# Loading q and k of the first three blocks in 512-byte pieces, and turning them head by head with the identity

## The chip, the core and the metric

The kernel runs on one core of one Trainium2 chip. The metric is the device time of one execution in microseconds (us). The core has five engines that run their own instruction queues in order: TensorE (PE, with its weight loads shown apart as PEld), VectorE (DVE), ScalarE (ACT), GpSimd (POOL) and SyncE (SP), which here issues nearly all DMAs.

## The reference

Three layers in a row. First an attention over 4 x 8 heads, 576 tokens, 64 columns a head, in which each token sees itself and the 63 before it; then a dense layer whose activation is a quotient of polynomials; then a layer of 8 experts, one per token.

```
scores = (1/8) * q @ k.T ;  rel = row - column ;  scores = where(0 <= rel < 64, scores, -1e9)
x  = softmax(scores) @ v                       # 2304 tokens x 512
h  = x @ w_in ;  g = P(h) / (Q(|h|) + 1e-6) ;  x = g @ w_out      # 512 -> 2048 -> 512
e  = argmax(x @ w_gate) ;  out = p[e] * sigmoid(x @ w_output_gate)[e] * relu(x @ w1[e]) @ w2[e]
```

q and k are float32, and the weights come as float64.

## The kernel before

The 2304 tokens are cut into nine blocks of 256 (`TB`). Attention works in units n = 4u + c: block u, and pair c of the eight heads. For two pairs at a time, m = n // 2 (block u, half g of the heads), `load_qk` (line 318) brings k and q into tiles of [128 partitions, 2, 4 heads, 64]: partition p and place t hold token 128t + p of the block. SP issues one DMA for each of k and q and each t; its pieces are the 64 floats of one token and head, 256 bytes. The first m is split into two pairs of heads more, which gives eight DMAs of 64 KB in place of four of 128 KB. In block 2 a sequence ends after 64 tokens, so its t = 0 takes two DMAs of 64 partitions.

`at_T` (line 407) turns a unit: four PE transposes (k and q, t = 0 and 1), each of a [128 tokens, 2 heads x 64] piece against the identity, into one PSUM tile `tq` of [128, 2, 2, 128]. Two evictions (`evac`, ACT or DVE) copy the k half into `kT`, and the q half, scaled, into `qT`, 256 tokens in a row for each of 128 head columns. kT and qT are parts of the one constant tile that the trace calls KK, so the evictions show as `KK<-tq`. Then `at_QK` (line 433) makes the scores: eight float32 matmuls a unit of 64 x 64 against 128 columns (`sc`); `soften` adds the mask (DVE), takes exponents (ACT) and scales (POOL, `ms<-ms,rs`); `at_PT` turns the result (`pp`, four transposes) and `at_PV` multiplies with v (`xp`, eight float32 matmuls of 128 x 64 against 64 columns).

Beside that run the conversion of w_in and w_out from float64 bits (`stg` -> `cp`, `ct` on DVE -> `wi`, `wo` on ACT and POOL) and the dense layer's first steps (`h`, `y`). All instructions from the start to step 12 (`S_TAPE`) of the dense layer are recorded by the class `Tape` and played in the order written out by hand in `ORDER` (line 36). That order fixes for each engine, SP too, what follows what, and for instructions with a choice the engine. The played instructions stand in the profile under line 124, all others under line 96. The units of the first three blocks (n = 0 to 11, u below `NG` = 3) and of block 3 lie in the played part; it ends on PE at about 84 us.

The order on PE around the turns is: turns 0 and 1, scores of 0 and 1; turns 2 and 3, `pp` of 0, scores of 2, `pp` of 1; turn 4, `xp`, scores, turn 5; later turns 6 and 7, then 8 and 9, then 10 and 11, with `xp`, `sc`, `pp` and `h` between them.

Of the kernel before, what the change touches and what calls it, by code (L numbers as in the profile page):

```python
# [23 lines left out]
NQ, TA, VU = 4, 2, 2  # L24
# [3 lines left out]
NG, HF = 3, 4  # L28
# [102 lines left out]
def kernel(  # L131
# [16 lines left out]
    nc = Tape(tc.nc)  # L148
    B, H, S, D = q.shape
# [3 lines left out]
    W = 64  # L153
    TB = 256
# [16 lines left out]
    scale = 1.0 / float(D) ** 0.5  # L171
# [33 lines left out]
    qT = [cols["qT"][:, i * TB:(i + 1) * TB] for i in range(NQ)]  # L205
    kT = [cols["kT"][:, i * (W + TB):(i + 1) * (W + TB)] for i in range(NP)]
# [3 lines left out]
    ident = cs[:, C_ID:C_ID + 128]  # L210
    qc_col = cs[:, C_QC:C_QC + 1]

    def t2(shape, name, dt=F32):
        return s2.tile(shape, dt, tag="s2", name=name)
# [7 lines left out]
    def pt(shape, name):  # L222
        return ps.tile(shape, F32, tag=name, name=name)
# [15 lines left out]
    def pick(**cost):  # L239
        e = min(cost, key=lambda x: load[x] + cost[x])  # L240
        load[e] += cost[e]
        return e

    def dve(n, fast=False):
        return 0.07 + n / (1920.0 if fast else 960.0)

    def act(n):
        return ACT0 + n / 1200.0
# [4 lines left out]
    def evac(o, i, n, mul=None):  # L253
        e = pick(D=dve(n), A=act(n))
        if mul is None:
            nc.either(e, D=lambda: nc.vector.tensor_copy(out=o, in_=i), A=lambda: nc.scalar.copy(out=o, in_=i))
        else:
            nc.either(e, D=lambda: nc.vector.tensor_scalar(out=o, in0=i, scalar1=mul, scalar2=None, op0=ALU.mult),
                      A=lambda: nc.scalar.mul(out=o, in_=i, mul=mul))
# [48 lines left out]
    def runs(t0, n):  # L308
        done = 0
        while done < n:  # L310
            b, s = divmod(t0 + done, S)
            step = min(n - done, S - s)
            yield done, step, b, s
            done += step
# [3 lines left out]
    def load_qk(m):  # L318
        u, g = divmod(m, 2)
        for nm, dst in (("k", k_t), ("q", q_t)):  # L320
            dst[m] = t2([128, 2, 4, D], nm)
        step = 4 if m else 2
        for h0 in range(0, 4, step):
            for src, dst in ((k, k_t[m]), (q, q_t[m])):
                for t in range(2):
                    for off, n, b, s in runs(u * TB + t * 128, 128):
                        h = 4 * g + h0
                        nc.sync.dma_start(out=dst[off:off + n, t, h0:h0 + step],
                                          in_=src[b, h:h + step, s:s + n, :].rearrange("h p d -> p h d"))
            if m == 0 and h0 == 0:  # L330
                nc.sync.dma_start(out=cs[:, C_MASK:], in_=cst[:, C_MASK:C_QC + 1])

# [74 lines left out]
    def at_T(n):  # L407
        nc.mark()
        u, c = divmod(n, NP)
        tq = pt([128, 2, 2, 128], "tq")  # L410
        cc = 2 * (c % 2)
        for a, src in ((0, k_t[n // 2]), (1, q_t[n // 2])):
            for r in range(2):
                nc.tensor.transpose(tq[:, a, r, :], src[:, r, cc:cc + 2, :].rearrange("p h d -> p (h d)"), ident)
        if u:
            e = pick(D=dve(W, True), A=act(W), G=0.2)
            nc.either(e if e == "G" else "D", G=lambda: nc.gpsimd.tensor_copy(out=kT[c][:, :W], in_=kT[c][:, TB:]),
                      D=lambda: nc.vector.tensor_copy(out=kT[c][:, :W], in_=kT[c][:, TB:]))
        evac(kT[c][:, W:], tq[:, 0].rearrange("d r p -> d (r p)"), TB)
        evac(qT[n % NQ], tq[:, 1].rearrange("d r p -> d (r p)"), TB, -scale)  # L420

    def mask(u, j):
        i = 4 * u + 2 * j
# [635 lines left out]
    def qk_upto(m):  # L1059
        while loaded[0] <= min(m, NUNIT // 2 - 1):  # L1060
            load_qk(loaded[0])
            loaded[0] += 1
# [8 lines left out]
    for n in range(NUNIT + 2):  # L1071
        first, second = [], []
        if n < NUNIT and (group(n) == 1 or n % 2):
            first.append((at_QK, n))
        if n % 2 and n > 2 and group(n - 2) == 2:
            first.append((at_PV, n - 2))
        if n + TA < NUNIT:
            second.append((at_T, n + TA))
        while done < min(n, NUNIT) and (group(done) == 1 or n % 2 == 0):
            first.append((at_PT, done))  # L1080
            if group(done) == 1:
                second.append((at_PV, done))
            done += 1
        evs += [first, second]
# [91 lines left out]
    for n in range(TA):  # L1176
        at_T(n)
# [158 lines left out]
```

## Time and profile before

| | us |
|---|---|
| median of 3 runs (753.07 to 754.02) | 753.62 |
| the profiled execution, its time | 752.35 |
| the profiled execution, its span (first to last instruction) | 750.60 |
| PE busy in the span | 726.9 |
| DVE, ACT, POOL busy | 509.9, 444.8, 461.7 |

PE busy counts instructions whose ends are modelled; a wait is what a view shows as idle time ahead of an instruction. A share of the DMA engines over 100% means that packets overlap in an engine.

### The profile page before, as it was taken

The numbers are of one execution on the slowest core, as the hardware profiler recorded it, in microseconds if no ns is written. First come the engines' busy times: TensorE is split into PE (matmuls) and PEld (weight loads), VectorE is DVE, ScalarE is ACT, GpSimd is POOL, SyncE is SP. The second block draws the span as 40 slices with busy tenths as digits, with TensorE's granted clock in tenths as the row PEclk, the third lists the DMA queues.
The fourth block names the chain that finished last, engine by engine and source line by source line (L and its number), as shares of the span: only waits on it lengthen the run. The fifth ranks groups of instructions, "written<-read, shape, count | busy, mean of one in ns | idle before, by whom it ended". The sixth has DMA issues, their size and how long they took to land.

```text
span 750.6 us, 14603 instructions
## 1 busy us (share of the span) xinstructions
PE 726.9 (97%) x5288; PEld 641.9 (86%) x5288; DVE 509.9 (68%) x1262; ACT 444.8 (59%) x1001; POOL 461.7 (62%) x390
## 2 busy tenths in 40 slices
PE   4889999999999999999999999999999999999996
PEld 3677998889899899899899999998888888888886
DVE  4999999987887867767767777798386622235111
ACT  4999776998577577577677566676531402223020
POOL 3588686665465665465475375577862867666451
PEclk9999999999999999999999999999999999999998
DMA  9999502433222022122121001146506545412410
GB/s 194 307 264 302 164 1 85 138 85 83 84 58 58 21 62 53 27 61 57 31 56 30 1 30 30 69 133 198 190 3 252 181 156 182 141 71 108 159 38 25
DMA packets 96865, 78.56 MB, mean 105 GB/s; under 512 B 74703, under 2 KB 75215, under 8 KB 96784
## 3 DMA queue, kind: packets, MB, share of 16 engines
q1 hardware_dynamic: 92944, 67.77, 30.9%
q0 software_dynamic: 3840, 9.76, 3.9%
q8 instruction: 44, 0.72, 0.4%
q14 instruction: 37, 0.30, 0.1%
HBM read 66.25 MB, written 11.53 MB: 104 GB/s over the span
## 4 chain that ended last, share of the span: by engine, by line
PE 84%; DMA 5%; DVE 4%; SPq 2%; ACT 2%; POOL 1%; issue 1%; POOLq 0%; DVEq 0%; ACTq 0%
PE y L96 20%; PE h L96 20%; PE hp L96 14%; PE yp L96 14%; PE h L124 3%; PE y L124 2%; SPq L124 2%; DMA q<-in_q_dram 2%; PE xp L96 1%; DVE t L96 1%; PE pp L96 1%; PE sc L96 1%; PE ytp L96 1%; DMA stg<-in_moe_w_out_dram 1%; PE lt L96 1%
## 5 line engine op out<-in xcount | busy, mean ns | idle before, releaser
L96 PE MATMUL y<-wo,g 128*128 128x512 f32 x768 | 190.1, 396 | 0.0
L96 PE MATMUL h<-xh,wi 128*128 128x256 f32 x896 | 171.7, 284 | 0.5 <-DVE mn L96 0.3
L96 PEld LDWEIGHTS y<-wo,g 128*128 128x128 f32 x768 | 139.6, 188 | 27.3 <-issue 0.2
L96 PEld LDWEIGHTS h<-xh,wi 128*128 128x128 f32 x896 | 143.6, 191 | 3.0 <-ACT ms L96 0.5
L96 PE MATMUL h<-xl,wi 128*128 128x256 f32 x448 | 127.5, 285 | 0.0
L96 POOL TENSOR_TENSOR wx<-wr,wx 128x1024 fp32r<-128x1024 f32 x44 | 107.0, 2460 | 26.6 <-DVE wx L96 17.8
L96 PE MATMUL yp<-wx,hT 128*128 128x512 f32 x432 | 99.3, 390 | 0.0
L96 POOL TENSOR_TENSOR g<-t,g 128x512 fp32r<-128x512 f32 x61 | 79.0, 1296 | 28.5 <-ACT g L96 27.5
L96 PEld LDWEIGHTS yp<-wx,hT 128*128 128x128 f32 x432 | 80.7, 188 | 16.6
L96 PEld LDWEIGHTS h<-xl,wi 128*128 128x128 f32 x448 | 85.7, 191 | 2.1
L96 POOL TENSOR_TENSOR qm<-qm,e 128x512 f32<-128x512 f32 x57 | 73.7, 1293 | 16.3 <-ACT qm L96 13.4
L96 PE MATMUL hp<-xbh,wx 128*128 128x512 f32 x256 | 80.3, 391 | 0.0
L96 DVE SCALAR_TENSOR_TENSOR t<-t,KK,r 128x512 f32<-128x512 f32 x61 | 45.4, 745 | 49.1 <-ACT r L96 48.4
L96 DVE SCALAR_TENSOR_TENSOR hT<-hp,hT 128x512 fp32r<-128x512 f32 x36 | 24.5, 687 | 54.0 <-ACT hT L96 54.0
L96 ACT ACTIVATE r<-qm,KK 128x512 f32<-128x512 f32 x61 | 42.2, 692 | 26.4 <-POOL qm L96 23.0
L96 PEld LDWEIGHTS hp<-xbh,wx 128*128 128x128 f32 x256 | 48.0, 188 | 9.8
L96 ACT ACTIVATE e<-h 128x512 f32<-128x512 f32 x60 | 35.8, 596 | 34.2 <-PE h L96 31.6
L96 ACT ACTIVATE hT<-hp 128x512 fp32r<-128x512 f32 x36 | 21.0, 596 | 56.1 <-PE hp L96 56.1
L96 POOL TENSOR_TENSOR ms<-ms,rs 128x512 f32<-128x512 f32 x24 | 24.9, 1041 | 46.5 <-DVE rs L96 28.2
L96 ACT CAST g<-t 128x512 fp32r<-128x512 f32 x62 | 38.4, 620 | 24.2 <-DVE t L96 17.7
L96 POOL TENSOR_SCALAR qm<-e,KK 128x512 f32<-128x512 f32 x34 | 26.4, 775 | 40.6 <-ACT e L96 34.7
L96 ACT ACTIVATE ob<-yp,tl 128x512 f32<-128x512 f32 x12 | 8.3, 690 | 71.5 <-PE yp L96 67.8
(221 smaller groups left out, 1587.7 us busy)
## 6 DMA issues: line engine op xcount, KB each, us to landing
wr<-in_moe_w_dram SPq DMA_DIRECT2D x48, 512.0 KB, 4.1
stg<-in_moe_w_in_dram SPq DMA_DIRECT2D x8, 1024.0 KB, 8.2
stg<-in_moe_w_out_dram SPq DMA_DIRECT2D x8, 1024.0 KB, 7.1
v<-in_v_dram SPq DMA_DIRECT2D x58, 128.0 KB, 2.9
k<-in_k_dram SPq DMA_DIRECT2D x30, 128.0 KB, 3.0
q<-in_q_dram SPq DMA_DIRECT2D x30, 128.0 KB, 3.0
y_dram<-ysb SPq DMA_DIRECT2D x12, 256.0 KB, 2.7
yp_dram<-yq SPq DMA_DIRECT2D x6, 256.0 KB, 2.2
```

The source lines that it names most:

```text
L96: return f(*a, **k)
L124: done = [f(*a, **k).ins for f, a, k in self.ops[n][1][e]]
```

## The change

For blocks 0 to 2 the tiles of q and k become [128, 4 heads, 2, 64], and partition p holds the two tokens 2p and 2p + 1 of the block. A piece is then two tokens of a head that follow each other in memory, 512 bytes, and a DMA for one t fills 64 partitions (in block 2's split ones, 32). Number, order and bytes of the DMAs stay. In `at_T` a transpose of two heads together is replaced by two float32 matmuls, one per head: the [128, 64] piece of one head and one token parity is the stationary operand, the identity the moving one, and the result goes to partitions 0 to 63 or 64 to 127 of `tq`. A result has even tokens (r = 0) and odd ones (r = 1) apart, so the two evictions read `tq` with r innermost, a step of 512 bytes from one element to the next, and write in a row as before. Blocks 3 to 8 keep the old way. `ORDER` is the same.

```diff
-            dst[m] = t2([128, 2, 4, D], nm)
+            dst[m] = t2([128, 4, 2, D] if u < NG else [128, 2, 4, D], nm)
...
-                        nc.sync.dma_start(out=dst[off:off + n, t, h0:h0 + step],
-                                          in_=src[b, h:h + step, s:s + n, :].rearrange("h p d -> p h d"))
+                        rows = src[b, h:h + step, s:s + n, :]
+                        if u < NG:
+                            p = (t * 128 + off) // 2
+                            nc.sync.dma_start(out=dst[p:p + n // 2, h0:h0 + step].rearrange("p h r d -> p h (r d)"),
+                                              in_=rows.rearrange("h (p r) d -> p h (r d)", r=2))
+                        else:
+                            nc.sync.dma_start(out=dst[off:off + n, t, h0:h0 + step],
+                                              in_=rows.rearrange("h p d -> p h d"))
...
-                nc.tensor.transpose(tq[:, a, r, :], src[:, r, cc:cc + 2, :].rearrange("p h d -> p (h d)"), ident)
+                if u < NG:
+                    for hh in range(2):
+                        nc.tensor.matmul(tq[64 * hh:64 * hh + 64, a, r, :], src[:, cc + hh, r, :], ident, start=True, stop=True)
+                else:
+                    nc.tensor.transpose(tq[:, a, r, :], src[:, r, cc:cc + 2, :].rearrange("p h d -> p (h d)"), ident)
...
-        evac(kT[c][:, W:], tq[:, 0].rearrange("d r p -> d (r p)"), TB)
-        evac(qT[n % NQ], tq[:, 1].rearrange("d r p -> d (r p)"), TB, -scale)
+        kt, qt = kT[c][:, W:], qT[n % NQ]
+        if u < NG:
+            evac(kt.rearrange("d (p r) -> d p r", r=2), tq[:, 0].rearrange("d r p -> d p r"), TB)
+            evac(qt.rearrange("d (p r) -> d p r", r=2), tq[:, 1].rearrange("d r p -> d p r"), TB, -scale)
+        else:
+            evac(kt, tq[:, 0].rearrange("d r p -> d (r p)"), TB)
+            evac(qt, tq[:, 1].rearrange("d r p -> d (r p)"), TB, -scale)
```

## Rows read from the trace of the kernel before

**Rows 1.** Stretch, length, PE, PEld, DVE, ACT, POOL busy; clock; DMA share; GB/s

```profile
13.60:19.66 6.06, 5.14 (x32) 3.86 (x33) 5.83 (x24) 4.01 (x14) 3.46 (x4) 1.00 1.14 213
...
24.00:41.70 17.70, 14.70 (x176) 12.34 (x176) 17.65 (x62) 17.46 (x63) 13.68 (x14) 1.00 1.06 312
41.70:62.00 20.30, 18.34 (x227) 15.83 (x226) 19.82 (x62) 19.44 (x59) 17.62 (x19) 1.00 1.01 262
...
104.00:750.60 646.60, 639.78 (x4446) 567.64 (x4444) 418.94 (x1004) 358.86 (x765) 389.29 (x303) 1.00 0.28 86
```

**Rows 2.** What PE waited for in the first 110 us: total, times, longest

```profile
PE tq L124 <- DMA k<-in_k_dram: 10.3, 3, 7.4
PE pp L124 <- POOL ms L124: 3.3, 3, 1.4
PE h L124 <- DVE ct L124: 1.2, 1, 1.2
PE y L124 <- DVE t L124: 0.6, 1, 0.6
```

**Rows 3.** PE in order of time: start, length, instructions, [idle before, releaser]

```profile
8.24 0.63 PE L124 MATMUL tq<-KK,k 128*128 128x128 f32 x2
8.67 0.63 PE L124 MATMUL tq<-KK,q 128*128 128x128 f32 x2
9.50 1.98 PE L124 MATMUL sc<-KK 64*64 64x128 f32 x32 [0.20 <-DVE KK L124]
...
14.87 0.47 PE L124 MATMUL tq<-KK,k 128*128 128x128 f32 x1 [0.73 <-DMA k<-in_k_dram]
15.47 0.69 PE L124 MATMUL tq<-KK,q 128*128 128x128 f32 x2
...
16.81 1.06 PE L124 MATMUL pp<-KK,ms 128*128 128x128 f32 x4
17.80 1.13 PE L124 MATMUL sc<-KK 64*64 64x128 f32 x16
...
19.72 0.38 PE L124 MATMUL tq<-KK,k 128*128 128x128 f32 x2
19.94 0.38 PE L124 MATMUL tq<-KK,q 128*128 128x128 f32 x2
20.25 0.69 PE L124 MATMUL xp<-ms,v 128*64 128x64 f32 x16
20.86 0.67 PE L124 MATMUL sc<-KK 64*64 64x128 f32 x16
```

**Rows 4.** DVE in order of time, 13 to 19 us

```profile
13.12 0.69 DVE L124 TENSOR_SCALAR cp<-stg 128x512 uint32<-128x512 uint32 x1 [1.42 <-DMA stg<-in_moe_w_in_dram]
...
19.02 0.29 DVE L124 CUSTOM_DVE_ANT_0 ms<-sc,KK 128x128 f32<-128x128 f32 x1 [0.23 <-PE sc L124]
```

**Rows 5.** DMA packets 13 to 18 us: count and bytes, rate, share of 16 engines

```profile
DMA packets 4365, 1.08 MB, mean 217 GB/s; under 512 B 4365, under 2 KB 4365, under 8 KB 4365
...
q1 hardware_dynamic: 4365, 1.08, 120.3%
```

**Rows 6.** The same, 67.54 to 67.97 us, almost alone the 512-byte pieces of `tf`

```profile
DMA packets 140, 0.07 MB, mean 151 GB/s; under 512 B 13, under 2 KB 140, under 8 KB 140
...
q1 hardware_dynamic: 140, 0.07, 58.5%
```

**Rows 7.** The same, 43.5 to 46 us, mostly block 2's pieces of 64 partitions

```profile
DMA packets 2020, 0.52 MB, mean 209 GB/s; under 512 B 2018, under 2 KB 2018, under 8 KB 2018
```

**Rows 8.** Evictions on ACT and a strided PSUM read on DVE: count, ns min/median/max

```profile
L124 ACT COPY KK<-tq x15: 350/373/414, 8.5 to 86.6; 128x256 f32<-128x256 f32 x15
...
L96 DVE TENSOR_REDUCE lgs<-lg x9: 214/225/226, 194.3 to 545.9; 128x32 f32<-128x64 f32 x9
```

**Rows 9.** The chain that ended last, first 110 us: start, us, what

```profile
27.19 8.73 DMA stg<-in_moe_w_out_dram
...
39.38 6.06 DMA v<-in_v_dram
```

## The prediction

> **What bounds the kernel now.** The busy times by stretch come first [rows 1]: after 104 us PE works 639.8 of 646.6 us, so whatever delays PE there reaches the end. Ahead of that no single engine bounds: from 24 to 62 us DVE is busy 17.65 of 17.70 and 19.82 of 20.30 us, ACT 17.46 and 19.44, and PE waits for them now and then. All instructions of that part run in an order written by hand, so a shift of DVE or ACT at 20 us is still there at 62 us, and PE, dense afterwards, carries it on. The second view is what PE waited for in the first 110 us [rows 2]: 10.3 us for k, of which 7.4 are the start itself; 1.4, 1.2 and 0.6 us are single waits for POOL and DVE later. Third, PE in order of time [rows 3]: the first turns stand at 8 us, the next wait for DMA until 15.47 us, and `pp` and `sc` follow. Fourth, DVE [rows 4]: it waits 1.42 us for the first weights until 13.12 us, then works almost without a gap; at 19.02 us it waits 0.23 us for the scores of unit 2. So the change can gain only where loads hold the start back, up to some 19 us, and can lose where PE, DVE or ACT have no gap.
>
> PE's speed matters for the early turns. The granted clock reads 1.00 in every stretch [rows 1], but the durations say otherwise: two transposes take 0.43 us at 8.24 us (to the next start at 8.67), and 0.22 us at 19.72 us. So PE runs at 1.2 GHz up to about 19.7 us and at 2.4 GHz from there, though it worked from 15.47 us on, and also, with a small gap, from 7.4 to 11.5 us, without the clock having risen in between [rows 3].
>
> **The loads.** In backlog a packet of 256 bytes occupies an engine for 120.3% x 16 x 5 us / 4365 = 22.0 ns, at 217 GB/s [rows 5]. Of 512 bytes there is one load: 58.5% x 16 x 0.43 us / 140 = 28.7 ns on average, 13 small ones among them, so at most 31.7 ns a piece [rows 6]. Ahead of the last q that turn 2 needs lie 1 MiB of q and k: 4096 packets of 22 ns now, 2048 of 31.7 then, or 5.63 and 4.06 us of each engine. Packets overlap by the factor 1.2 that the share shows, so the upper end of the gain is 1.3 us. The lower end is slightly below nothing: block 2's pieces, which fill 64 partitions instead of 128, moved at 209 GB/s [rows 7] against 217 [rows 5], and every DMA of the changed loads fills 64 or fewer; 4% of 4.8 us is a loss of 0.2 us. The 512-byte row is one of 128 partitions and without backlog, the 64-partition row one of 256 bytes; neither is nearer, and I take the middle, 0.6 us.
>
> The Trainium skill (SBUF — State Buffer, Door 1: the DMA port swizzle) speaks against the change here: 64 partitions in a row reach eight of the sixteen ports of SBUF, about half the rate, and two DMAs on the two halves hardly add up. By it the loads would gain nothing; the 209 GB/s of rows 7 fit it, but 256-byte packets of all 128 partitions are no faster than 217, so no row of before can tell it from a cost per packet.
>
> The number of DMA issues stays, so SP's instructions are the same; where an issue blocks on a full queue, half as many packets can only shorten it.
>
> **The turns.** A transpose is one instruction; a float32 matmul shows as two, since `sc` has 32 for the sixteen matmuls of two units [rows 3]. A turn goes from 4 instructions to 16. The nearest row is `xp`: eight matmuls of 128 x 64 weights in two halves, x16, from 20.25 to 20.86 us, 0.61 us [rows 3]. Its moving side has 64 columns, the identity 128. Ends: 0.61 us if the columns cost nothing, 1.22 if everything doubles. I take 0.9, since the streaming doubles but the changeover from the work before, which is in the 0.61, does not. A turn took 0.44 us; it costs 0.46 more at 2.4 GHz, and 0.9 more at 1.2 GHz (transposes there took 0.86, so the new form 1.8). Eight fast turns and four slow ones add 8 x 0.46 + 4 x 0.9 = 7.3 us of PE. What reaches the end:
> - Turns 0 and 1: 1.8 us before the first scores at 9.50 us [rows 3]. Behind them DVE waits 1.42 us for the weights [rows 4], and the first loads land a few tenths earlier; I count 0, at worst 0.4.
> - Turns 2 and 3: a matmul contracts over all 128 partitions, so the first needs both loads of k, the second in at 14.87 us. From there k of turn 2 takes 0.9, q 0.9, turn 3 1.8: 18.47 us, where `pp` now begins at 16.81 us [rows 3], or 1.66 us later. Loads 0.6 us sooner leave 1.06. PE's steady run also begins sooner, so that the clock rises within `pp` and `sc` and not after them: I take back 0.5 (at most half of the 2 us that these two take). 0.55 us remain, and DVE at 19.02 us, already waiting for `sc`, has no slack [rows 4].
> - Turns 4 to 9: 6 x 0.46 = 2.8 us. After 6 and 7 `pp` waits 1.4 us for POOL, after 8 and 9 `h` waits 1.2 us for DVE [rows 2]; each covers 0.92. Turns 4 and 5 lie in a stretch where PE waits for others, too. I count 0; without cover it is 2.8.
> - Turns 10 and 11 (about 50 us): 0.92 us in a stretch without gaps, up to a wait of 0.64 us for DVE [rows 2]: 0.28 us.
>
> **The evictions.** 24 copies of 256 elements, nearly all on ACT at 373 ns [rows 8], now read PSUM with a step of 512 bytes. Fewer elements are not read, so no gain; the upper end is the whole length again, 0.37 us each. The nearest strided read of PSUM is DVE's `lgs<-lg`, 64 elements in 225 ns at a step of 64 bytes [rows 8]; no stall is seen there, though most of 225 ns may be fixed cost. I take 0.
>
> **Sum.** 0.55 + 0.28 = 0.8 us later. On the profiled execution that is a span of 751.4 for 750.60 and a time of 753.15 for 752.35; the median of the runs lies 1.27 us above that execution, so I forecast 753.62 + 0.8 = 754.4 us, own range 753.4 to 755.6. A measurement can tell 0.2%, 1.5 us: 752.1 to 755.1 counts as no change.
>
> **Rivals.**
> - *The clock rises sooner.* Turns 0 and 1 and their scores now make PE busy for some 5.5 us almost in one go, where 4.1 us did not raise the clock [rows 3]. If it rises then, turns 2 and 3 cost 0.9 each at 2.4 GHz: k in at 14.27, q at 14.87, done at about 16.2 us, 0.6 before now. DVE gains no more than its weights land earlier, some 0.5 us. With +0.28 from turns 10 and 11: 753.4. For it: the longer run; against: gaps of half a us for the evictions stay.
> - *The strided evictions run at half rate* (slower). The place is ACT from 20 to 53 us, where the 16 evictions of turns 4 to 11 lie and ACT has next to no gap [rows 1]; the price is some 0.2 us each (half of 373 ns and a little), 3.2 us with 0.8 of the forecast: 757.6. It decides from 0.05 us per eviction on, which makes 0.8 us and with the forecast's own 0.8 passes 755.1. For it: 512 bytes is far beyond the 64 of the only strided row; against: that row.
> - *Half the ports.* Loads no faster than now, so turns 2 and 3 cost 1.66 - 0.5: 1.16 + 0.28 gives 755.1, with the 0.2 us loss 755.3. The Trainium skill's rule on ports, named above, is this case. It holds as well if the pieces go out as 256 bytes after all, so that the change does not do what it says.
> - *The loads bound further than 19 us.* The chain of waits runs through a load of w_out (27.19 us, 8.73 long) and of v (39.38, 6.06 long) [rows 9]. If so, all six loads count: 6144 pairs x (44 - 31.7 ns) / 16 / 1.2 = 3.9 us less, 750.5. Against it: DVE and ACT busy all through that stretch [rows 1]; the chain names the last of several that end together.
>
> **Chances.** Forecast 0.47; clock 0.17; evictions 0.13; ports 0.17; loads 0.06. Faster by over 0.2%: the loads and a small part of the clock's case, 0.10. Slower: evictions, 0.10 of the ports' case and 0.08 of the forecast's upper end, 0.31. The same: 0.59. The range 752.2 to 757.6 leaves out the loads' case, the upper half of the evictions' and the far ends of the others.
>
> **What would show it.** In the changed trace: packets of 512 bytes at 28 to 32 ns and a rate over 217 GB/s from 13 to 18 us, or not; `tq` with x16 a turn and 0.9 us from its start to the next group at 2.4 GHz; when the last q of turn 3 is turned and at which clock; the mask work of unit 2 on DVE some 0.5 us after 19.02; evictions still at 373 ns; the waits of 1.4, 1.2 and 0.6 us shrunk. It is wrong if the instructions after the played part, whose order a planner makes, come out in another order; if neighbouring halves do not run side by side, which doubles a turn; or if turns 4 and 5 hold ACT up.

## The result, and the profile after

The changed kernel takes 757.70 us (median of 5 runs, 756.89 to 759.28), the kernel before beside it 753.10 (752.62 to 754.02): a ratio of 1.0064, interval 1.0048 to 1.008. It is 4.6 us slower; the forecast was 754.4. The profiled execution took 757.70 us, with a span of 756.0.

The loss is made before 90 us. Two lines of the turns' last group, before and after (count, ns, first and last start in us): from the last turn to the end of the span there are 750.6 - 84.4 = 666.2 us before and 756.0 - 89.6 = 666.4 us after, so what was lost by then is what the end shows.

```profile
L96 PE MATMUL tq<-KK,q x2: 273/273/273, 84.2 to 84.4; 128*128 128x128 f32 x2
```

```profile
L96 PE MATMUL tq<-KK,q x2: 272/272/273, 89.4 to 89.6; 128*128 128x128 f32 x2
```

What PE waited for in the first 110 us of after, against [rows 2]: the waits for k have grown from 10.3 to 13.0 us, q has come in with 1.4, and the waits for POOL and DVE have shrunk (3.3 to 1.3, 1.2 to 0.2, 0.6 to 0.4). PE comes late enough for those to be ready.

```profile
PE tq L124 <- DMA k<-in_k_dram: 13.0, 3, 7.3
PE tq L124 <- DMA q<-in_q_dram: 1.4, 2, 1.1
PE pp L124 <- POOL ms L124: 1.3, 2, 0.7
PE y L124 <- DVE t L124: 0.4, 1, 0.4
PE h L124 <- DVE ct L124: 0.2, 1, 0.2
```

PE in order of time, after, for [rows 3]: k of unit 2 is waited for until 16.45 us (14.87 before), `pp` begins at 19.80 (16.81), and a second wait for k, of unit 6, stands at 31.28 us, where before turn 6 began at 27.18 us without one (the last line, of before).

```profile
7.25 1.12 PE L124 MATMUL tq<-KK,k 128*64 128x128 f32 x8 [7.25 <-DMA k<-in_k_dram]
8.13 1.10 PE L124 MATMUL tq<-KK,q 128*64 128x128 f32 x8
9.02 1.07 PE L124 MATMUL tq<-KK,k 128*64 128x128 f32 x8
...
16.45 0.66 PE L124 MATMUL tq<-KK,k 128*64 128x128 f32 x8 [3.80 <-DMA k<-in_k_dram]
...
19.80 1.00 PE L124 MATMUL pp<-KK,ms 128*128 128x128 f32 x4
...
21.92 0.66 PE L124 MATMUL tq<-KK,k 128*64 128x128 f32 x8
22.41 0.61 PE L124 MATMUL tq<-KK,q 128*64 128x128 f32 x8
22.84 0.64 PE L124 MATMUL xp<-ms,v 128*64 128x64 f32 x16
...
31.28 1.12 PE L124 MATMUL tq<-KK,k 128*64 128x128 f32 x8 [1.98 <-DMA k<-in_k_dram]
```

```profile
27.18 0.72 PE L124 MATMUL tq<-KK,k 128*128 128x128 f32 x2
```

DVE in after, for [rows 4]: it waits for the first weights until 14.64 us, not 13.12. These weights are an unchanged load.

```profile
14.64 0.69 DVE L124 TENSOR_SCALAR cp<-stg 128x512 uint32<-128x512 uint32 x1 [1.88 <-DMA stg<-in_moe_w_in_dram]
```

The DMA packets of after from 14 to 17 us (count, rate, share of 16 engines), for [rows 5]: nearly all are the new 512-byte pieces. One occupies an engine for 122.7% x 16 x 3 us / 1344 = 43.8 ns, double the 22.0 of a 256-byte piece before, and the rate is 216 GB/s as it was 217.

```profile
DMA packets 1344, 0.65 MB, mean 216 GB/s; under 512 B 77, under 2 KB 1344, under 8 KB 1344
...
q1 hardware_dynamic: 1344, 0.65, 122.7%
```

Then SP's own issues of the first 12 us (count, ns min/median/max, first and last start), three lines of before and the same three of after. In after an issue of q takes 610 ns and not 468. One of v takes 596 ns and one of `stg` 595, where both took 468, though nobody changed these loads. And w_in's first load, `stg`, goes out at 8.4 us and not at 7.0.

```profile
L124 SPq DMA_DIRECT2D q<-in_q_dram x6: 368/468/507, 1.8 to 9.9; - x6
L124 SPq DMA_DIRECT2D v<-in_v_dram x2: 467/468/469, 3.3 to 5.4; - x2
L124 SPq DMA_DIRECT2D stg<-in_moe_w_in_dram x1: 468/468/468, 7.0 to 7.0; - x1
```

After:

```profile
L124 SPq DMA_DIRECT2D q<-in_q_dram x6: 601/610/734, 1.8 to 11.0; - x6
L124 SPq DMA_DIRECT2D v<-in_v_dram x2: 594/596/597, 3.8 to 6.4; - x2
L124 SPq DMA_DIRECT2D stg<-in_moe_w_in_dram x1: 595/595/595, 8.4 to 8.4; - x1
```

Last, the stretch in which these issues go out, 6 to 10 us, of before and of after (columns as [rows 1]). Before, the DMA engines are busy for 0.98 of it and move 217 GB/s; after, for 0.55, at 132 GB/s. Here the engines have too little queued, whatever a piece costs.

```profile
6.00:10.00 4.00, 2.43 (x19) 2.03 (x23) 1.29 (x4) 1.45 (x4) 0.00 (x0) 1.00 0.98 217
```

```profile
6.00:10.00 4.00, 2.75 (x24) 2.32 (x24) 0.43 (x2) 1.06 (x3) 0.00 (x0) 1.00 0.55 132
```

### The profile page after: what moved, and what is told of

Read it like the earlier page. It is cut to its first block, busy times and chain, and to the rows that moved or that the text cites. A ratio compares the mean times of both kernels' runs of the same rounds, so it can differ in the third digit from the quotient of the medians.

```text
span 756.0 us, 14881 instructions
## 1 busy us (share of the span) xinstructions
PE 731.9 (97%) x5432; PEld 647.6 (86%) x5432; DVE 512.4 (68%) x1262; ACT 445.0 (59%) x1001; POOL 461.7 (61%) x390
## 4 chain that ended last, share of the span: by engine, by line
PE 81%; DVE 6%; DMA 5%; SPq 2%; POOL 2%; ACT 2%; issue 1%; POOLq 0%; DVEq 0%
PE y L96 20%; PE h L96 19%; PE hp L96 14%; PE yp L96 14%; PE y L124 2%; PE h L124 2%; SPq L124 2%; DMA q<-in_q_dram 2%; PE xp L96 1%; DVE t L96 1%; DMA stg<-in_moe_w_out_dram 1%; DMA stg<-in_moe_w_in_dram 1%; PE pp L96 1%; PE sc L96 1%; PE ytp L96 1%; DVE t L124 1%
## 5 line engine op out<-in xcount | busy, mean ns | idle before, releaser
L96 POOL TENSOR_TENSOR g<-t,g 128x512 fp32r<-128x512 f32 x61 | 79.1, 1296 | 28.7 <-ACT g L96 27.6
```

Of the source, the lines that this page charges most:

```text
L96: return f(*a, **k)
```

## The experiments

First question: is it the turns (theory B) or the loads (theory A), and if the loads, is it that each DMA fills 64 partitions? Second: what about 64 partitions costs, the transfers or SP's issues? Times in us; "k of unit 2" is when turn 2 has waited for its last k, "turn 6" when it starts; issue is the median of q's in the first 12 us (in merged two of the four are longer, 0.63 and 1.92 us). All columns from issue on are of the one profiled execution, the time is the median of all.

| kernel | time | ratio to before, interval | issue | w_in's load out | k of unit 2 | turn 6 | last turn |
|---|---|---|---|---|---|---|---|
| before | 753.10 | | 0.47 | 7.0 | 14.87 | 27.18 | 84.4 |
| after | 757.70 | 1.0064, 1.0048 to 1.008 | 0.61 | 8.4 | 16.45 | 31.28 | 89.6 |
| after_beside (the same) | 757.37 | 1.0041, 1.0014 to 1.0067 | 0.61 | 8.4 | 16.38 | 30.88 | 86.6 |
| after_again (the same) | 757.64 (one run) | | 0.61 | 8.4 | 16.33 | 31.29 | 88.7 |
| turns_only | 753.57 | 0.998, 0.996 to 1.0 | 0.49 | 7.0 | 14.63 | 28.28 | 86.6 |
| loads_only | 756.91 (one run) | | 0.61 | 8.3 | 17.56 | 30.39 | 88.6 |
| full_partitions | 752.03 | 0.9961, 0.9941 to 0.9981 | 0.47 | 6.7 | 13.17 | 26.37 | 83.6 |
| ports_again (the same) | 751.75 | 0.9979, 0.9959 to 0.9999 | 0.47 | 6.7 | 13.01 | 26.34 | 83.3 |
| even_odd | 755.28 | 1.001, 1.0001 to 1.002 | 0.61 | 8.4 | 15.87 | 28.86 | 89.0 |
| even_odd_again (the same) | 755.01 | 1.002, 0.9993 to 1.0047 | 0.61 | 8.4 | 16.13 | 29.12 | 86.3 |
| block0_only | 758.23 | 1.0045, 1.0028 to 1.0062 | 0.61 | 8.3 | 17.75 | 30.80 | 89.0 |
| both | 755.35 (one run) | | 0.47 | 6.7 | 12.99 | 27.04 | 86.7 |
| merged | 751.70 | 0.9975, 0.9962 to 0.9988 | 0.57 | 4.9 | 13.68 | 26.83 | 83.7 |
| one_head | 758.29 | 1.0057, 1.0036 to 1.0077 | 0.43 | 6.7 | 13.88 | 30.92 | 90.5 |

Three cautions for reading it. Executions of one kernel differ by a few us (after_beside from 754.92 to 760.1, and it was the 754.92 that was profiled; of even_odd the 757.46, its slowest), so times are compared as medians and traces for where a wait stands. The median of before moved between 753.10 and 754.66 from set to set, so a time is best read as its ratio, or against a kernel of its own set. And turn 2 needs both DMAs of k where each brings half of the tokens; where a DMA brings all tokens of one head or more (full_partitions, ports_again, both, merged, one_head), the k of turn 2 stands earlier in the queue, so that its column favours these five. The q of turn 2 needs its last DMA in all of them and says the same, for full_partitions with a smaller number: 15.47 us before, 17.07 in after, 14.43 in full_partitions.

**turns_only**: the old loads, the new turns (against before).

```diff
-                nc.tensor.transpose(tq[:, a, r, :], src[:, r, cc:cc + 2, :].rearrange("p h d -> p (h d)"), ident)
+                if u < NG:
+                    for hh in range(2):
+                        nc.tensor.matmul(tq[64 * hh:64 * hh + 64, a, r, :], src[:, r, cc + hh, :], ident, start=True, stop=True)
+                else:
+                    nc.tensor.transpose(tq[:, a, r, :], src[:, r, cc:cc + 2, :].rearrange("p h d -> p (h d)"), ident)
```

> Old loads (256-byte pieces, 128 partitions), turns of blocks 0 to 2 by float32 matmuls head by head; evictions read in a row as before. Theory A (the loss comes from loads that arrive later, the turns are mostly covered): k of unit 6 is no longer late (turn 6 starts by 28.5 us against 31.28 in the changed kernel and 27.18 before), turn 2 starts at 15 us, and the kernel is 0.5 to 2 us slower than before, not 4.6. Theory B (the loss is the PE time of the turns, 7.3 us more of which most is not covered): 4 to 5 us slower than before, as the whole change.

753.57, ratio 0.998, at most 1.0: beside the old loads the turns cost nothing that shows in the time. Turn 4 begins at 19.58 us, 0.14 earlier than before, although turns 2 and 3 take longer. Theory B falls. The trace by itself would not say so: its last turn stands 2.2 us behind that of before, but it is of an execution of 754.75 us and that of before of one of 752.35.

**loads_only**: the new loads, and transposes that take the two tokens of one head together (against after).

```diff
-                    for hh in range(2):
-                        nc.tensor.matmul(tq[64 * hh:64 * hh + 64, a, r, :], src[:, cc + hh, r, :], ident, start=True, stop=True)
+                    nc.tensor.transpose(tq[:, a, r, :], src[:, cc + r, :, :].rearrange("p r d -> p (r d)"), ident)
```

> New loads (512-byte pieces, two tokens a partition, 64 partitions a DMA), but four transposes a turn as before; each takes a head's two tokens together, so that units 0 to 11 get their columns in the wrong places and the later routing sees other values: read only up to the end of the played part, where the last turn stood at 84.2 us before and 89.2 us in the changed kernel. Theory A: k of unit 2 lands at about 16.4 us and k of unit 6 at about 31 us, as in the changed kernel; the end of the played part at 87 to 89 us. Theory B: 84 to 85 us. SP's issues: if the pattern of 64 partitions makes them long, 0.60 us each up to 16 us as in the changed kernel, otherwise 0.50.

One run of 756.91 us, issues of 0.61 us, k of unit 2 even later than in after (17.56). The loss comes with the loads. Its size is not clean: this kernel also has a wait that neither before nor after has, told under both, and why its k comes 1.1 us later than in after stays open.

**full_partitions**, and once more as **ports_again**: 512-byte pieces and matmul turns as in the change, but a DMA fills all 128 partitions with half of the heads.

```diff
+                if u < NG:
+                    parts = list(runs(u * TB, TB))
+                    hs = step // 2
+                    for off, n, b, s in parts:
+                        split = ((0, step),) if len(parts) == 2 and off == 0 else ((0, hs), (hs, step))
+                        for x0, x1 in split:
+                            h = 4 * g + h0
+                            rows = src[b, h + x0:h + x1, s:s + n, :]
+                            p = off // 2
+                            nc.sync.dma_start(out=dst[p:p + n // 2, h0 + x0:h0 + x1].rearrange("p h r d -> p h (r d)"),
+                                              in_=rows.rearrange("h (p r) d -> p h (r d)", r=2))
+                    continue
...
-                            p = (t * 128 + off) // 2
-                            nc.sync.dma_start(out=dst[p:p + n // 2, h0:h0 + step].rearrange("p h r d -> p h (r d)"),
-                                              in_=rows.rearrange("h (p r) d -> p h (r d)", r=2))
```

> The changed kernel, but a DMA fills all 128 partitions with 512-byte pieces of half of the heads, where the changed one fills 64 partitions with all of them; as many DMAs and bytes (in block 2: 32, 96 and 96 partitions). Theory A1 (64 partitions reach half of the ports, the Trainium skill, SBUF State Buffer, Door 1): the rate from 13 to 16 us rises from 220 to 270 to 300 GB/s and a 512-byte packet falls from 44 to some 32 ns, unit 2's k lands 1 us sooner, and the kernel is within 1.5 us of before. Theory A2 (512-byte pieces cost what two of 256 do, whatever the partitions): 220 GB/s and 44 ns stay, and it is 3 to 5 us slower than before.

> The kernel with DMAs over all 128 partitions and half of the heads (512-byte pieces, turns by matmuls) a second time, beside the others of this set. If its gain is real, 752 to 752.6 us and a ratio of 0.996 to 0.998, k of unit 2 in by 13.2 to 13.7 us and k of unit 6 waiting for nothing. If the first look was luck, a ratio of 0.999 to 1.001.

752.03 and 751.75 us: faster than before by 0.4% and 0.2%, so it beats both kernels. The packets of 12 to 14 us, of before and of full_partitions:

```profile
DMA packets 1960, 0.50 MB, mean 249 GB/s; under 512 B 1954, under 2 KB 1954, under 8 KB 1960
...
q1 hardware_dynamic: 1960, 0.50, 126.9%
```

```profile
DMA packets 1294, 0.63 MB, mean 313 GB/s; under 512 B 77, under 2 KB 1292, under 8 KB 1294
...
q1 hardware_dynamic: 1294, 0.63, 118.3%
```

A 512-byte piece costs 118.3% x 16 x 2 us / 1294 = 29.3 ns here, inside the 28.7 to 31.7 that the prediction read from `tf`, against 43.8 in after: the pieces are good, what they fill is not. Theory A1, then, but the gain is larger than it said: k of unit 2 comes 3.3 us sooner than in after and not 1, and the kernel beats before. SP's issues are short again, too, and A1 had no term for that.

**after_again**: the changed kernel itself.

> The changed kernel once more, for what belongs to the kernel and what to one execution: SP's issues of 0.60 us up to 16 us, k of unit 2 at 16.45 us, k of unit 6 at 31.28 us, and the two falls of the clock at 17.1 and 30.8 us. If they belong to the kernel, each is there again within 0.5 us.

757.64 us; k of unit 2 at 16.33 us and a wait of 2.13 us for k of unit 6, until 31.29. The issues and both waits for k are there again, within 0.2 us. The fall of the clock at 30.8 us is not, as the part on the prediction shows.

**even_odd**, and beside the changed kernel **even_odd_again** and **after_beside**: as the change, with 64 partitions a DMA, but every second one.

```diff
+                            p, e = off // 2, (off + n) // 2
...
+                                nc.sync.dma_start(out=dst[p + t:e:2, h0:h0 + step].rearrange("p h r d -> p h (r d)"),
+                                                  in_=rows.rearrange("h (p x r) d -> x p h (r d)", x=2, r=2)[t])
...
-                            p = (t * 128 + off) // 2
-                            nc.sync.dma_start(out=dst[p:p + n // 2, h0:h0 + step].rearrange("p h r d -> p h (r d)"),
-                                              in_=rows.rearrange("h (p r) d -> p h (r d)", r=2))
```

> The changed kernel with one difference: of the two DMAs for a tensor the first fills the even partitions and the second the odd ones, 64 partitions each, where the change fills 0 to 63 and 64 to 127. Pieces (512 bytes), partitions per DMA, bytes, count and order of the DMAs stay (block 2: 32 partitions in a row, then the even and the odd ones of the other 96). Theory P: what costs time is that 64 partitions in a row lie in one half; every second partition of 128 has no such half. Then the kernel goes as the one with DMAs over all 128 partitions: packets of 512 bytes near 27 to 34 ns where the changed kernel has 44 to 49, SP's issues of q and k near 0.43 to 0.47 us and not 0.60, k of unit 2 in by 13.2 to 13.8 us, last turn of the played part at 83 to 85 us, and a time of 752 to 753.5 us (ratio 0.996 to 0.999). Theory N: it is the number of partitions that a DMA fills, whichever they are. Then it goes as the changed kernel: 44 to 49 ns, 0.60 us an issue, k of unit 2 at 16.3 us, 757 to 758 us (ratio 1.005 to 1.007). The Trainium skill (SBUF — State Buffer, Door 1: the DMA port swizzle) speaks for P: by its table of ports the even partitions reach all sixteen.

> The kernel with even and odd partitions a second time, beside the changed kernel, to split the loss between the two causes. Two causes (the long issues of DMAs of 64 partitions, and the slower packets of 64 partitions in a row): 754.5 to 756 us, ratio 1.000 to 1.002, issues of 0.60 us, k of unit 2 at 15.5 to 16 us, packets of 512 bytes near 32 ns. One cause, the issues alone: the same time as the changed kernel beside it, within 0.5 us.

> The changed kernel itself on the same chip: 757 to 758.3 us, ratio 1.004 to 1.007, issues of 0.60 us, k of unit 2 at 16.3 to 16.5 us, packets near 46 ns. The difference to the even and odd partitions, 1.5 to 3 us, is then what the slower packets cost; what the even and odd partitions lose against the DMAs over all 128 partitions (751.7), some 3 us, is what the issues cost.

Neither theory P nor theory N of the first expectation: half of each. The packets became fast and the issues stayed long. First even_odd_again's packets from 14 to 17 us, 108.5% x 16 x 3 us / 1817 = 28.7 ns each (230 small ones among them) at 283 GB/s, then SP's issues, then 6 to 10 us:

```profile
DMA packets 1817, 0.85 MB, mean 283 GB/s; under 512 B 230, under 2 KB 1815, under 8 KB 1817
...
q1 hardware_dynamic: 1817, 0.85, 108.5%
```

```profile
L124 SPq DMA_DIRECT2D q<-in_q_dram x6: 606/611/759, 1.8 to 11.0; - x6
L124 SPq DMA_DIRECT2D stg<-in_moe_w_in_dram x1: 594/594/594, 8.4 to 8.4; - x1
```

```profile
6.00:10.00 4.00, 2.43 (x20) 2.06 (x22) 0.71 (x2) 0.48 (x2) 0.00 (x0) 1.00 0.59 131
```

So there are two causes, and each has its place. From 6 to 10 us the DMA engines lack work as in after, at 131 GB/s, although these pieces are fast: (217 - 131) GB/s x 4 us = 0.34 MB less than before, an estimated 1.2 us at 283 GB/s. It fits the delay at turn 2: k of unit 2 is late by 1.0 and 1.3 us in the two executions (15.87 and 16.13 for 14.87). The slow packets add 0.3 to 0.6 us there, and at turn 6, where after and after_beside wait 1.98 and 1.27 us for k, even_odd waited 0.5 us and even_odd_again not at all.

How the loss of time divides is less sure. Beside each other after_beside took 757.37 and even_odd_again 755.01, so the slow packets are worth some 2.4 us, though the intervals of their two ratios overlap. Beside each other even_odd took 755.28 and ports_again 751.75, so some 3.5 us are left to the issues; but these two differ in the heads that a DMA brings as well.

**block0_only**: the change for block 0 alone (shown is the loads' line; the tile's shape, the turns and the evictions change likewise).

```diff
-                        if u < NG:
+                        if u < 1:
```

> The change for block 0 alone (loads of 64 partitions and matmul turns for units 0 to 3); blocks 1 and 2 load and turn as before. Theory S: the loss is made at the start and only carried on. Then turn 2 is late by 2.5 to 3 us and the time is that of the changed kernel, 756.5 to 757.7 us (ratio 1.005 to 1.006). Theory L: the loads of block 1 bind a second time, at turn 6 (4.1 us late in the changed kernel, of which 2 us stood before it). Then turn 2 is as late as in the changed kernel, k of unit 6 comes by 29.3 us and not 31.3, and the time is 754.8 to 756 us (ratio 1.002 to 1.004). The prediction's own assumption, that loads hold only the first 19 us, fits S alone.

758.23 us, ratio 1.0045. Turn 6 begins at 30.80 us without any wait for k, so nearly all of the delay was there before block 1's loads: theory S for this kernel, with turn 2 late by 2.9 us and the time 0.5 us above the range it gave. Its k of unit 2 comes 1.3 us later than in after, though the loads of block 0 are the same; why stays open, as in loads_only. It does not clear block 1's loads in the changed one, since here they are 256-byte pieces over all partitions. And some of it is the wait told under both.

**both**: the loads of full_partitions, the transposes of loads_only.

> 512-byte pieces over all 128 partitions, and turns by four transposes a unit as before; a transpose takes the two tokens of one head together, so that the columns of units 0 to 11 stand in other places than they should. It tells what the matmul turns cost once the loads are early. Theory A: nothing, the turns lie beside other waits: k of unit 2 at 13.2 us as with matmul turns, scores of units 2 and 3 on DVE earlier by up to 1 us but the last turn of the played part at 83 to 84.2 us, span 749.3 to 750.5 us. Theory B: the matmul turns cost the 0.8 us of the prediction, or more: last turn at 81.5 to 82.8 us, span 748 to 749 us.

Fast loads (k of unit 2 at 12.99), yet 755.35 us in its one run and the last turn at 86.7, later than with the dearer turns. Neither theory said so. What ACT waited for from 30 to 46 us in both and in ports_again:

```profile
ACT t L124 <- POOL wi L124: 1.9, 1, 1.9
ACT ms L124 <- PE pp L124: 0.2, 1, 0.2
```

```profile
ACT ms L124 <- PE pp L124: 0.2, 1, 0.2
```

ACT's first `t<-h` waits 1.9 us for a POOL conversion. From turn 6 to turn 8 it is 14.5 us in both (27.04 to 41.52) and 13.1 in ports_again (26.34 to 39.41). The same wait stands in loads_only and block0_only, and neither in before nor in after. The order of instructions on PE is the same, so what moved is what the instruction has to wait for; that the buffer of `t` came to lie elsewhere is the likely reason, but only argued. It makes loads_only, block0_only and both some 1.4 us too dear, and leaves open what the turns cost beside fast loads.

**merged** and **one_head**: full_partitions with half as many issues (both halves of the heads in one DMA), and with twice as many for units 2 to 7 (one head a DMA).

```diff
-                        split = ((0, step),) if len(parts) == 2 and off == 0 else ((0, hs), (hs, step))
+                        split = ((0, step),)
```

```diff
-                        for x0, x1 in split:
+                        for x0, x1, more in ([(x, x + 1, x % 2) for x in range(step)] if m and u < 2
+                                             else [(x0, x1, 0) for x0, x1 in split]):
```

> As the kernel with DMAs over all 128 partitions and half of the heads, but the two halves in one DMA: 128 partitions, 4 heads (2 for the first unit pair), 512-byte pieces, half as many issues on SP for q and k of blocks 0 to 2, the same packets. Theory I: the length and number of SP's issues carry part of the loss, since the loads of weights and of v stand behind them. Then w_in's first load goes out at 4.7 to 5.3 us and not at 6.69, the last q of unit 2 at 6 to 7 us and not at 9.15, k of unit 2 is in by 12 to 13.2 us and the time is 750 to 751.5 us. Theory R: behind the ports only the rate of the transfers counts. Then k of unit 2 is in at 13 to 13.4 us and the time is 751.3 to 752.3 us. It also tells what lengthens an issue: if one DMA over 128 partitions of 4 heads takes 0.43 to 0.51 us, the 0.60 us of the changed kernel belong to its 64 partitions; if 0.60 or more, to four pieces of 512 bytes in a partition.

> The other way: all 128 partitions and one head a DMA for units 2 to 7 (blocks 0 and 1), which makes eight issues in place of four for two units; packets, bytes and their order in memory stay as in the kernel with half of the heads. It puts the issues where the changed kernel has them (last q of unit 2 at 11 us) without its 64 partitions. Theory I: k of unit 2 comes at 14.3 to 15.9 us, the last turn of the played part at 84.5 to 87 us and the time is 753 to 755.3 us, as with the even and odd partitions (755.28). Theory R: k of unit 2 at 13 to 13.6 us and 751.3 to 752.5 us.

The two frame the issues' part. merged sends w_in's load out at 4.9 us, 1.8 sooner than full_partitions, and gains nothing (751.70): theory R by the time, though its k of unit 2, at 13.68, lies beyond both theories. From 6 to 10 us its DMA engines are busy for 1.06 of the stretch, so there the transfers bind. one_head loses 6.6 us against it (758.29). SP's queue and then the packets from 13 to 17 us in one_head, and the same packets in before:

```profile
7.16 0.98 SPq L124 DMA_DIRECT2D k<-in_k_dram  x2
8.18 1.91 SPq L124 DMA_DIRECT2D q<-in_q_dram  x2
10.13 0.91 SPq L124 DMA_DIRECT2D k<-in_k_dram  x2
11.08 2.81 SPq L124 DMA_DIRECT2D q<-in_q_dram  x2
```

```profile
DMA packets 849, 0.39 MB, mean 96 GB/s; under 512 B 96, under 2 KB 849, under 8 KB 849
...
q1 hardware_dynamic: 849, 0.39, 34.6%
```

```profile
DMA packets 3503, 0.87 MB, mean 218 GB/s; under 512 B 3503, under 2 KB 3503, under 8 KB 3503
...
q1 hardware_dynamic: 3503, 0.87, 119.9%
```

With 64 KB an issue the DMA engines stand at 34.6% and 96 GB/s, starved by SP: theory I in that direction. It is not the issues' length alone: SP also waits 2.0 us for the landing of w_in's first load before its eighth issue behind it. full_partitions waits there, too, for 1.4 us, but with DMAs twice as large it has queued more by then. What SP waited for in the first 20 us, in one_head and in full_partitions:

```profile
SPq L124 <- DMA stg<-in_moe_w_in_dram: 2.0, 1, 2.0
```

```profile
SPq L124 <- DMA stg<-in_moe_w_in_dram: 1.4, 1, 1.4
```

Its k of unit 2 was not as late as expected (13.88 for 14.3 to 15.9), turn 6 was late (30.92), behind waits for k and q, and the time lies 3 us above theory I's range. So in these kernels issues longer or more than the transfers need are paid for; fewer ones gain nothing.

merged tells also what lengthens an issue: for the first unit pairs its DMA has 128 partitions with two 512-byte pieces each and takes 0.43 to 0.51 us, the change's has 64 partitions with the same two pieces and takes 0.60 to 0.73. It goes with the 64 partitions, in a row or not, and not with the pieces.

## Why the prediction was wrong, by its own steps

- **What bounds the kernel**: right in the main. The 666 us behind the played part stayed within 1.5 us in every kernel, and what was left of a delay at the last turn came out at the end. But part of a delay can be made up on the way: after_beside starts turn 6 3.7 us later than before, and its last turn 2.2 us later.
- **The loads**: the failed term. It stood at a gain of 0.6 us, the middle of +1.3 and -0.2. Measured, k of unit 2 is 1.6 us later and k of unit 6 is waited for again. Two steps of it failed.
  - *"SP's instructions are the same"*: they are the same in number, not in length. Ten issues stand ahead of w_in's first load, each some 0.14 us longer: the 1.4 us by which it leaves late. Only the count was argued; the length of an issue was not bounded from both sides, as the other unseen costs were.
  - *The middle between the two ends*: the 64-partition row [rows 7] was the nearer one. 512-byte pieces cost 43.8 ns and moved at 216 GB/s, which is that end; the 31.7 ns of [rows 6] hold where all 128 partitions are filled (29.3 in full_partitions). The Trainium skill (SBUF — State Buffer, Door 1: the DMA port swizzle) gives eight of sixteen ports for 64 partitions in a row, and by its table every second partition reaches all sixteen. The runs agree in the direction, 43.8 ns in a row and 28.7 with every second one; in size the 216 GB/s are some 70 to 76% of the 313 and 283, and not half.
- **The turns**: sizes right, reach wrong. A turn takes 22.84 - 21.92 = 0.92 us at 2.4 GHz and, by its doubled durations at 1.2 GHz, 9.02 - 7.25 = 1.77, for 0.9 and 1.8. Of the 0.8 us that were to reach the end nothing shows in turns_only (0.998, at most 1.0). The part taken back for a clock that rises sooner was too small. In turns_only `pp` begins 0.99 us later than before, but `pp`, `sc` and `pp` then take 19.58 - 17.80 = 1.78 us at 2.4 GHz where they took 19.72 - 16.81 = 2.91 at 1.2: 1.13 us given back and not 0.5, so that turn 4 starts 0.14 us sooner. The lines of turns_only:

```profile
17.80 0.66 PE L124 MATMUL pp<-KK,ms 128*128 128x128 f32 x4
...
19.58 0.66 PE L124 MATMUL tq<-KK,k 128*64 128x128 f32 x8
```

- **The evictions**: right. In after ACT's copies out of `tq` take 372 ns where [rows 8] have 373:

```profile
L124 ACT COPY KK<-tq x15: 350/372/424, 9.3 to 91.9; 128x256 f32<-128x256 f32 x15
```

- **The rivals**: *half the ports* was the right mechanism for the transfers, at 755.1 to 755.3 too small by 2.4 us, since it had neither the issues nor the wait at turn 6. *The loads bound further than 19 us* was set aside because DVE and ACT have no gap there [rows 1]; true for faster loads (merged gains nothing more), not for slower ones: at turn 6 the slack of k was used up and became a wait of 1.98 us. The argument worked in one direction only, and the forecast used it for both. *The clock rises sooner* came about in ports_again, where k of turn 3 takes 0.44 us (14.78 to 15.22), but not in after: there the granted clock is 0.51 from 17.1 to 20 us, and k of turn 3 takes 0.85 (17.94 to 18.79).
- **The clock**: not foreseen is that it can fall again behind a wait of PE. The granted clock and the busy times of after, of after_beside and of after_again from 30.8 to 34.2 us (columns as [rows 1]):

```profile
30.80:34.20 3.40, 2.92 (x28) 2.95 (x30) 3.10 (x11) 1.92 (x7) 2.28 (x2) 0.50 1.13 344
```

```profile
30.80:34.20 3.40, 3.22 (x52) 2.60 (x52) 3.40 (x13) 3.09 (x13) 2.42 (x3) 1.00 1.13 343
```

```profile
30.80:34.20 3.40, 2.91 (x52) 2.60 (x52) 3.40 (x13) 2.68 (x9) 2.28 (x2) 1.00 1.13 346
```

After has 0.50, 1.2 GHz, behind its wait of 1.98 us for k; after_beside, with a wait of 1.27 us at the same place, and after_again, with one of 2.13, keep 1.00. The longest of the three waits kept its clock; what decides it stays open. From turn 6 to turn 8 after takes 44.50 - 31.28 = 13.2 us and the two others 11.9 and 11.8: the fall costs some 1.3 us there. By itself it does not explain how executions differ: after_again, without it, took 757.64 us, nearly the 757.70 of after, and after_beside 754.92.

## What to carry to other kernels

Cost a DMA by what it fills as well as by the size of its pieces: longer pieces paid here (29 ns for 512 bytes against 21 to 22 for 256) in time only once each DMA filled all 128 partitions, and splitting by heads in place of tokens kept the number of issues and turned 0.6% slower into 0.2 to 0.4% faster. Treat the queue that issues DMAs as an engine with durations of its own: read the length of its issues, not only their number, and look at what stands behind them. And an argument that a load is hidden holds only as far as its slack reaches, so ask it for a later load as well as for an earlier one.

## What the hardware did that was not expected

- An issue on SP of a DMA that fills 64 partitions took 0.60 us against 0.43 to 0.51 with 128, and the issues of unchanged loads between them grew alike (v: 468 to 596 ns). Why the neighbours grow stays open.
- 512-byte pieces cost 43.8 ns with partitions 0 to 63 or 64 to 127, 28.7 with the even or the odd ones, 29.3 with all 128.
- The granted clock fell to 1.2 GHz and rose again after the start, in places that differ between executions of one kernel (0.50 from 30.8 to 34.2 us in after, 1.00 in after_again).
- A wait of 1.9 us of ACT for POOL came and went with edits that don't touch the instructions concerned, as both shows.
